# Gate preparation of an mLSTM kernel on 80 rows, and its state decay as a step of its own

## The chip, the cores and the metric

The kernel runs on one core of one Trainium2 chip. The metric is the device time of one execution in microseconds. TensorE (PE), VectorE (DVE), ScalarE (ACT), GpSimd (POOL) and SyncE (SP) work side by side, and semaphores order them.

## The reference

Three layers follow each other. The first is an mLSTM attention over 2 batches, 8 heads, 768 steps and 40 channels a head; then come two dense blocks on 1536 tokens of 320 channels.

```
for t in range(S):
    m_new = max(f[t] + m, i[t])
    f_stab, i_stab = exp(f[t] + m - m_new), exp(i[t] - m_new);  m = m_new
    C = f_stab * C + i_stab * outer(v[t], k[t])
    n = f_stab * n + i_stab * k[t]
    y[t] = sigmoid(o[t]) * (C @ q[t]) / max(abs(n . q[t]), 1)
x = rows of y                      # 1536 x 320
x = (((x @ w1) * (x @ w2)) @ w3) @ w_out        # inner width 1024
h = x @ w_in                                    # inner width 2048
out = (h * tanh(softplus(h))) @ w_out2
```

## The kernel before, in words

The sequence is cut into 6 chunks of 128 steps. A unit is one chunk of one batch with all 8 heads, so there are 12 units; two chunks form a block of 512 tokens, and the dense layers work on 3 blocks. Inside a chunk the recurrence is written as products: E builds the exponents of the weights (lines 624 and, for the first `mu` = 8 units, a product that adds the causal mask, line 623; later units are masked by GpSimd in `ms`, line 634). `dw` takes exp of them, S is the product of keys and queries (line 650), `wg` multiplies both on VectorE, and Y (line 699) applies the result to the values. What earlier chunks contribute goes through a state `st`: I (line 661) applies the state to the queries, `Ie` scales the result with `eT`, and `cb` adds Y. U (line 675) makes what the unit adds to the state. `state()` first multiplies the old state with the decay `d` (which `dx` computes from a row of I) and then adds U, all on VectorE. `vw` (GpSimd) scales the values for U. `r1` to `r3`, `xs` and `xo` make the output row, X turns it over, and `Xe` and `Xl` split it into a high and a low part.

The gates are prepared in `start()`, in three stages: chunk 0, chunk 1 and chunks 2 to 5. Sixteen sequences of (batch, head) lie on 128 rows, eight times repeated, since E needs them at several row ranges: a scan gives the running maximum m (`pa`, line 879), two subtractions make the exponents (`pt`), a clamp and a scan sum them up (`pb`, `pc`, line 900). `lr` and `ll` write the sums L as a high and a low part to rows 64 to 127, `less`, `la` and `lb` (lines 927, 931, 935) write the left factor `ex_l` of E, `rb` and `rc` the right factor `ex_r` (VectorE or ScalarE), `turn` transposes L and `turned` takes exp of it into `eT` (lines 943 and 947).

The dense layers run in fp32r with three products of high and low parts. Each weight piece comes in by a load (`raw`), and is split on ScalarE, VectorE and GpSimd (lines 487 to 512 and the `lo` step); A and B are the products with w1 and w2 (line 1057), W makes w3 times w_out ahead of time (line 1028), X1 applies it, H and O are the two products of the last layer (lines 1186 and 1210), which alternate in groups of 8.

The order of every instruction on every engine is written out before the kernel is built: the steps are nodes with an engine, an assumed duration, a due number, the nodes they need and the places (PSUM banks b0 to b7, SBUF slots) that they take. `Work.plan` lists them one after the other, at each step the node that is due first among those that could start soon; `DUE` holds the due numbers and `TUNE` the rest. Where the plan sees TensorE idle while units still run, it puts in fillers: `keep_warm` (line 594), a product of 512 columns into bank b0 that nobody reads. Loads are issued by SP in plan order. What `port=True` marks are steps that the plan keeps apart in time on VectorE and GpSimd.

Of the kernel before, what the change touches and what calls it, by code (L numbers as in the profile page):

```python
# [19 lines left out]
NQK = 2  # L20
# [24 lines left out]
    set_0=0.0, ld_o_0=0.6, ld_g=1.3, ld_qk_0=1.7, ld_kv_0=1.8, load_0=1.9, ld_o_1=4.6, lr_0=4.8, less_0=2.3,  # L45
    ll_0=4.5, la1_0=5.1, la0_0=5.4, rb_0=5.6, one_0=5.7, lb0_0=40.7, lb1_0=6.2, pl_1=6.1, rc_0=6.4, pl_0=18.6,
    E_0=5.8, pa_1=7.7, pr_1=15.4, pa_2=7.8, E_1=7.5, dw_0=8.0, ld_qk_1=8.7, pt_1=9.7, S_0=9.2, pt_2=9.4,
    ld_kv_1=23.2, pb_1=10.6, dw_1=7.0, pb_2=11.3, pc_1=11.4, pc_2=11.7, te_1=16.7, lr_1=11.5, turn_1=7.0,
    less_1=13.1, te_2=11.7, lr_2=24.7, less_2=13.8, load_1=14.8, turn_2=13.5, ll_2=13.9, la1_2=13.7, ll_1=14.5,
    sgm_0=14.3, ld_o_2=24.2, vw_0=4.4, lb1_2=13.6, U_0=-11.7, ld_qk_2=16.0, rb_1=11.7, wg_0=16.2, la0_2=16.4,  # L50
    sgm_1=17.3, vw_1=16.8, ld_kv_2=16.6, la1_1=16.9, st_0=17.9, Y_0=-10.7, la0_1=13.8, mag_0=16.9, lb0_2=18.8,
    lb0_1=19.0, set_1=19.1, lb1_1=-2.1, rc_1=19.4, S_1=19.3, clamp_0=20.0, rb_2=20.1, cb_0=20.6, load_2=18.4,
    E_2=18.1, wg_1=21.0, xs_0=23.9, r1_0=19.4, mag_1=20.5, E_3=22.0, ld_o_3=20.4, r2_0=17.9, bits1_0=11.3,
    dw_2=20.6, U_1=22.5, r3_0=27.8, bits2_0=25.1, Y_1=22.8, ld_qk_3=23.3, st_1=23.8, xo_0=31.7, bits_0=26.7,
    ld_kv_3=26.0, dw_3=23.6, S_2=24.4, cb_1=24.0, vw_2=24.7, r1_1=24.3, I_2=-2.3, rc_2=25.2, wg_2=26.2, U_2=27.2,
    xs_1=31.5, dx_2=25.6, dup_0=23.1, Ie_2=29.8, hi_0=26.6, E_4=28.1, load_3=16.7, st_2=38.2, Y_2=28.6, dw_4=29.5,
    r2_1=28.5, lo_0=28.6, r3_1=29.2, mag_2=24.8, clamp_1=29.0, xo_1=29.9, X_0=13.8, ld_qk_4=30.2, cb_2=28.4,
    E_5=24.6, Xe_0=29.1, clamp_2=24.8, dup_1=32.5, r1_2=29.7, Xl_0=24.4, xs_2=30.9, S_3=32.8, dw_5=29.1,
    ld_kv_4=62.5, r2_2=27.1, bits1_2=28.7, ld_o_4=32.5, I_3=33.4, r3_2=32.2, vw_3=33.1, bits2_2=27.0, X_1=47.3,
# [1287 lines left out]
```

## Time and profile before

| | us |
|---|---|
| median of 3 runs | 418.37 (418.22 to 418.58) |
| the profiled execution | 418.2 |
| its span, first to last instruction | 416.5 |
| TensorE busy | 409.5 (98%) |
| VectorE busy | 291.1 (70%) |
| ScalarE busy | 197.7 (47%) |
| GpSimd busy | 80.4 (19%) |

The 70% of VectorE is a mean over unlike stretches. In the first 110 us, where the units run, it is busy nearly all the time; from 300 us on it has little to do. The chain of waits that ended last is 93% TensorE and 5% VectorE, and VectorE's share of it lies in the first 20 us, and a little around 70 us.

### The profile page before, as it was taken

How to read it: one execution, taken by the hardware profiler on the slowest of the kernel's cores; microseconds unless marked ns; L12 is line 12 of the kernel's file. 1: busy time of each engine (PE TensorE's matmuls, PEld its weight loads, DVE VectorE, ACT ScalarE, POOL GpSimd, SP SyncE). 2: the span in 40 equal slices, each digit the busy share in tenths (PEclk: the TensorE clock that was granted, in tenths of full speed). 3: DMA queues.
4: the chain of work that ended last, by engine and by line, in shares of the span. 5: the costliest groups of instructions: out<-in, count | busy, mean ns of one | idle time of the engine just before them, and what ended most of it. 6: DMA issues, size and time to landing. Idle time of an engine off the chain costs nothing.

```text
span 416.5 us, 7129 instructions
## 1 busy us (share of the span) xinstructions
PE 409.5 (98%) x2815; PEld 359.8 (86%) x2815; DVE 291.1 (70%) x527; ACT 197.7 (47%) x381; POOL 80.4 (19%) x78
## 2 busy tenths in 40 slices
...
GB/s 238 324 178 220 239 119 153 139 97 127 114 50 102 168 136 101 150 139 166 65 104 87 64 127 90 164 63 2 65 0 2 0 2 2 63 2 0 2 2 64
DMA packets 30497, 40.88 MB, mean 98 GB/s; under 512 B 1856, under 2 KB 24640, under 8 KB 30464
## 3 DMA queue, kind: packets, MB, share of 16 engines
...
q10 hardware_dynamic: 512, 0.48, 0.4%
...
## 4 chain that ended last, share of the span: by engine, by line
PE 93%; DVE 5%; DMA 1%; ACT 0%; issue 0%; DVEq 0%
PE pso L1210 21%; PE psh L1186 20%; PE psb L1057 11%; PE psa L1057 10%; PE psw L1028 7%; PE psY L699 5%; PE psS L650 3%; PE psx L1097 3%; PE psx L1099 3%; PE psx L1098 3%; PE psI L661 2%; PE psx L1102 1%; PE psx L1101 1%; PE psE L624 1%; DVE gates L410 1%; PE psX L743 1%
## 5 line engine op out<-in xcount | busy, mean ns | idle before, releaser
L410 DVE TENSOR_TENSOR gl<-u,gh 128x512 fp32r<-128x512 f32 x48 | 32.9, 691 | 68.7 <-ACT u L1195 68.7
L1191 ACT ACTIVATE gh<-psh 128x512 fp32r<-128x512 f32 x48 | 28.8, 601 | 79.5 <-PE psh L1186 79.4
L1186 PE MATMUL psh<-xd,wih 64*128 64x512 f32 x240 | 59.4, 395 | 0.0
L1186 PEld LDWEIGHTS psh<-xd,wih 64*128 64x128 f32 x240 | 43.1, 184 | 3.6 <-ACT u L1195 0.2
L1210 PE MATMUL pso<-wo,gh 128*128 128x320 f32 x192 | 42.6, 310 | 0.0
L1186 PE MATMUL psh<-hs,wih 64*128 64x512 f32 x144 | 41.6, 395 | 0.0
L502 DVE SCALAR_TENSOR_TENSOR f<-raw,f 128x640 int32<-128x640 int32 (+2 forms) x44 | 40.0, 908 | 0.9
L507 DVE SCALAR_TENSOR_TENSOR f<-raw,f 128x640 int32<-128x640 int32 (+2 forms) x44 | 37.7, 858 | 0.9
L410 POOL TENSOR_TENSOR th<-f,th 128x512 fp32r<-128x512 f32 x16 | 22.1, 1381 | 62.1 <-ACT th L512 59.1
L1210 PEld LDWEIGHTS pso<-wo,gh 128*128 128x128 f32 x192 | 32.0, 188 | 1.1 <-issue 1.1
L1186 PE MATMUL psh<-xd,wil 64*128 64x512 f32 x120 | 31.6, 391 | 0.0
L1186 PE MATMUL psh<-hs,wil 64*128 64x512 f32 x120 | 31.4, 391 | 0.0
L1210 PE MATMUL pso<-wo2h,gh 128*128 128x320 f32 x96 | 30.0, 312 | 0.0
L1210 PE MATMUL pso<-wo2h,gl 128*128 128x320 f32 x96 | 29.6, 309 | 0.0
L1210 PE MATMUL pso<-wo2l,gh 128*128 128x320 f32 x96 | 29.6, 309 | 0.0
L1210 PE MATMUL pso<-wo,gl 128*128 128x320 f32 x96 | 29.6, 309 | 0.0
L1057 PE MATMUL psa<-hs,w12h 128*128 128x512 f32 x72 | 28.9, 401 | 0.1
L1195 ACT ACTIVATE u<-psh 128x512 f32<-128x512 f32 x48 | 28.9, 603 | 0.0
L1057 PE MATMUL psb<-hs,w12h 128*128 128x512 f32 x72 | 28.3, 394 | 0.2 <-DVE y L410 0.2
L1186 PEld LDWEIGHTS psh<-hs,wih 64*128 64x128 f32 x144 | 25.7, 184 | 3.2 <-issue 1.3
L1028 PE MATMUL psw<-woh,th 128*128 128x320 f32 x128 | 28.5, 310 | 0.0
L493 DVE TENSOR_SCALAR f<-f 128x640 f32<-128x640 f32 (+2 forms) x44 | 23.6, 536 | 7.0 <-ACT f L487 6.3
...
## 6 DMA issues: line engine op xcount, KB each, us to landing
...
```

The source lines that it names most:

```text
L410: return eng.tensor_tensor(out=o, in0=a, in1=b, op=op)
L493: nc.vector.tensor_scalar(out=ff, in0=ff, scalar1=HI_MIN, scalar2=HI_MAX, op0=ALU.max, op1=ALU.min)
L502: nc.vector.scalar_tensor_tensor(out=f, in0=t["raw"][:, :, 1], scalar=-0x40000000, in1=f, op0=ALU.bitwise_and, op1=ALU.bitwise_or)
L507: nc.vector.scalar_tensor_tensor(out=f, in0=t["raw"][:, :, 0], scalar=29, in1=f, op0=ALU.logical_shift_right, op1=ALU.bitwise_or)
L650: nc.tensor.matmul(t["S"][g][:, p * T:(p + 1) * T], lhsT=t["qk"][rows, 1, p, :], rhs=t["qk"][rows, 0, p, :], start=True, stop=True)
L699: nc.tensor.matmul(ps[:, h * VW:(h + 1) * VW], lhsT=t["w"][:, h, :], rhs=t["v"][:, h, :], start=True, stop=True)
L1028: nc.tensor.matmul(ps, lhsT=t[a][:, 0, c * 128:(c + 1) * 128], rhs=wo[b], start=(c0 + c + s == 0), stop=(c0 + c == KC - 1 and s == 2))
L1057: nc.tensor.matmul(ps, lhsT=a, rhs=b, start=(n == 0 and not begun), stop=(n == len(seq) - 1))
L1186: nc.tensor.matmul(mt[i + k]["ps"], lhsT=w[k][:, c], rhs=x[k][c], start=(n == 0 and c == 0), stop=(n == 2 and c == KC2 - 1))
L1191: nc.scalar.activation(out=t["gh"], in_=t["ps"], func=AF.Mish)
L1195: nc.scalar.activation(out=t["u"], in_=t["ps"], func=AF.Mish)
L1210: nc.tensor.matmul(ps, lhsT=t[a][:, sl], rhs=wo[b], start=(ft == 0 and n == 0), stop=(ft == KF2 - 1 and n == 2))
```

## The change

The gates of chunk 0 stay as they were. For chunks 1 to 5 the running maximum is one scan over 640 columns on the 16 distinct rows. Then each (chunk, sequence) gets a row of its own, 80 rows of 128 columns: the gates are loaded a second time in this form (`cf`, `ci`), and the maxima are placed on the 80 rows by five products with a selecting matrix (`mv`, into PSUM). Subtractions, clamp, sum and `less` run once on 80 rows. The results are split in high and low parts (`chi`) and placed back on the rows that E needs by products with a second selecting matrix (`rp`, in groups of two chunks), from where ScalarE and VectorE copy them out of PSUM (`evL`, `ev0`, `ev1`). One transpose replaces five. The loads of the gates of chunks 1 to 5 are four transfers in place of two, of 16 or 80 rows in place of 128.

The decay of the state becomes the node `sd`; `ENG` puts it on GpSimd for units 2 to 9, the units that have one. `r2` of unit 5 goes to GpSimd as well. `mu` is 9, so one more unit takes the causal mask from TensorE. The plan gets a bonus `fb` for a TensorE node of the same form as the one before, fills idle time to 0.901 rather than 0.972, and adds fillers where a stretch would have too few wide products (`gd` = 0.26). A unit's Y is listed behind X of four units earlier. In the last block the slots of the second layer's results may also lie in buffers that are free by then, and the output tiles take others. `DUE` is new for most early nodes, and the added nodes have entries. With `ss` = 9 and `grp` = (0, 8, ..., 48) S stays one node a unit and H and O alternate in groups of 8. The old stages' functions, shown above, are gone; below are the added lines and those of the old ones that they replace elsewhere.

```diff
-    sgg=(2, 4), mu=8, s_pe=0.268, s_act=0.543, s_dve=0.435, s_pool=0.206, ahead=1, w0n=5, ff=0.972, gd=0.0,
+    sgg=(2, 4), mu=9, s_pe=0.268, s_act=0.563, s_dve=0.435, s_pool=0.1, ahead=1, w0n=5, ff=0.901, gd=0.26,
     ph=0.071, a0=-12.81, ap=-93.853, a_ld=-1652.39, e_e=8363.2, e_s=3345.95, e_r=2252.59, g_ld=6316.58,
...
+                    stay = TUNE["fb"] if e == "PE" else 0.0
+                    c = min((c for c in cand if c[0] <= s0 + TUNE.get(SLACK.get(e), 0.0)),
+                            key=lambda c: c[1] - (stay if self.form[c[2]] == form else 0.0))
...
+        if tag[0] == "y":
+            k, n = divmod(int(tag[1:]), 5)
+            h, l = xset["b", k]
+            return (h[:, n] if n < 3 else l[:, n - 3]).bitcast(F32)
...
+        sd_e = ENG.get(f"sd{u}", ENG["sd"])
+
+        def sd():
+            s = st[b].rearrange("a p (e v) -> a (p e) v", e=2)
+            tt(nc.gpsimd if sd_e == "POOL" else nc.vector, s, s, t["d"].unsqueeze(2).to_broadcast([128, H, VW]), mult)
+
         def state():
...
-            if c > 0:
-                s = st[b].rearrange("a p (e v) -> a (p e) v", e=2)
-                tt(nc.vector, s, s, t["d"].unsqueeze(2).to_broadcast([128, H, VW]), mult)
...
+        g = (c - 1) // 2 if c else 0
+        node("E", "PE", -K["e_e"], 0.92 if pe_mask else 0.46, E, [(f"ev{b}" if c else f"lb{b}", g), ("rb", c), ("rc", c), ("E", u - 1)],
...
-                node("dx", "ACT", -1, 0.08, dx, [("I", u)], [(places("d", 2), [("st", u)])], table=["exp"])
+                node("dx", "ACT", -1, 0.08, dx, [("I", u)], [(places("d", 2), [("sd", u)])], table=["exp"])
+                node("sd", sd_e, -1, pool(328) if sd_e == "POOL" else dve(328), sd, [("I", u), ("dx", u)], port=True)
             st_a = c == 0 and ENG["st0"] == "ACT"
-            node("st", "ACT" if st_a else "DVE", -1, 2 * act(164) if st_a else (dve(328) if c else 0.0) + 2 * dve(164), state,
-                 [("U", u), ("I", u), ("dx", u)])
-        node("Y", "PE", 0, 1.8, Y, [("wg", u), ("ld_kv", u)], [at("cb")], warm=0.31)
+            node("st", "ACT" if st_a else "DVE", -1, 2 * act(164) if st_a else 2 * dve(164), state,
+                 [("U", u), ("sd", u)] if c else [("U", u)])
+        node("Y", "PE", 0, 1.8, Y, [("wg", u), ("ld_kv", u), ("X", u - 4)], [at("cb")], warm=0.19)
...
+        CF = 1
+        NK = NCH - CF
+        S1 = S - CF * T
+        NC = G * NK
...
+        m, one, L, sel_m = part(gb, S + 1, T, F, 2 * NC - G)
+        cf, ci, cL = [x[0:NC] for x in part(gc, T, T, T)]
+        chi = z_a.tile([128, N], F32R, tag="z3", name="split", bufs=1)[0:NC]
+        sel_m = sel_m[0:G]
         L2 = xs.tile([128, 2, N], F32R, tag="ls2", name="gates", bufs=1).rearrange("a c n -> a (c n)")[:, 0:S]
+        sel_r = z_a.tile([128, N], F32R, tag="z2", name="sel", bufs=1)[0:NC, 0:176]
...
+        def prep_sel():
+            nc.gpsimd.memset(sel_m, 0.0)
+            nc.gpsimd.tensor_copy(out=sel_m[:, NC - G:NC], in_=ident[0:G, 0:G])
+            nc.gpsimd.memset(sel_r.bitcast(F32), 0.0)
+            for a in range(0, NC, 32):
+                r = slice(a, min(a + 32, NC))
+                n = r.stop - a
+                nc.gpsimd.tensor_copy(out=sel_r[r, 32:160].rearrange("a (h q) -> a h q", h=2)[:, :, 0:n],
+                                      in_=ident[r, r].unsqueeze(1).to_broadcast([n, 2, n]))
...
+        def gate_max(c):
+            a, z = c * T, (c + 1) * T
+            nc.vector.tensor_tensor_scan(out=m[:, a + 1:z + 1], data0=f[:, a:z], data1=i[:, a:z], initial=m[:, a:a + 1],
+                                         op0=add, op1=ALU.max)
+
+        def gate_diff(f, i, m_before):
+            tt(nc.vector, f, f, m_before, add)
+            tt(nc.vector, i, f, i, sub)
+
+        def gate_sum(f, i, L, skip=0):
+            nc.vector.tensor_scalar(out=f, in0=i, scalar1=0.0, scalar2=-120.0, op0=ALU.min, op1=ALU.max)
+            nc.vector.tensor_tensor_scan(out=L[:, skip:], data0=one[0:L.shape[0], skip:], data1=f[:, skip:], initial=0.0,
+                                         op0=mult, op1=add)
+
+        def less(i, L):
+            nc.vector.scalar_tensor_tensor(out=i, in0=i, scalar=0.0, in1=L, op0=ALU.max, op1=add)
+
+        def cut(a, c):
+            return a[:, c * T:(c + 1) * T]
+
+        gate_max(0)
+        gate_diff(cut(f, 0), cut(i, 0), cut(m, 0))
+        nc.vector.memset(L[:, 0:1], 0.0)
+        gate_sum(cut(f, 0), cut(i, 0), cut(L, 0), 1)
+
+        def ld_c():
+            for o, a in ((f1, f_gate), (i1, i_gate)):
+                nc.sync.dma_start(out=o, in_=a[0:G, F:S])
+            for o, a in ((cf, f_gate), (ci, i_gate)):
+                nc.sync.dma_start(out=o, in_=by_chunk(a[0:G, F:S]))
+
+        gps = {}
+
+        def mv():
+            gps["m"] = bank("psg")
+            for c in range(NK):
+                a = F + c * T
+                nc.tensor.matmul(gps["m"][0:NC, 0:T], lhsT=sel_m[:, NC - G - c * G:2 * NC - G - c * G], rhs=m[0:G, a:a + T],
+                                 start=(c == 0), stop=(c == NK - 1))
+
+        def group(n):
+            return range(2 * n, min(2 * n + 2, NK))
+
+        def rp(n):
+            gps["r", n] = bank("psg")
+            r = slice(32 * n, min(32 * n + 32, NC))
+            for c in group(n):
+                o = gps["r", n][:, c % 2 * 2 * T:(c % 2 + 1) * 2 * T]
+                for e in range(2):
+                    a = 32 + c % 2 * G - 32 * e
+                    nc.tensor.matmul(o, lhsT=sel_r[r, a:a + 128], rhs=chi[r, 2 * e * T:2 * (e + 1) * T], start=(e == 0), stop=(e == 1))
+
+        def copied(n, k):
+            w = len(group(n))
+            o = slice(F + 2 * n * T, F + (2 * n + w) * T)
+            return o, gps["r", n][:, 0:2 * w * T].rearrange("a (c k t) -> a c k t", c=w, k=2)[:, :, k]
+
+        def flat(o):
+            return o.rearrange("a (c t) -> a c t", t=T)
+
+        def ev_eng(nm, n):
+            return ENG[f"{nm}{n}"]
+
+        def evL(n):
+            sl, a = copied(n, 0)
+            o, a = flat(L2[64:128, sl]), a[64:128]
+            nc.scalar.copy(o, a) if ev_eng("evL", n) == "ACT" else nc.vector.tensor_copy(out=o, in_=a)
+
+        def ev(b, n):
+            sl, a = copied(n, 1)
+            o, a = flat(ex_l[b][0:64, sl]), a[0:64]
+            if ev_eng(f"ev{b}", n) == "ACT":
+                nc.scalar.activation(out=o, in_=a, func=AF.Copy, scale=neg_b[:, b:b + 1])
+            else:
+                nc.vector.tensor_scalar_mul(out=o, in0=a, scalar1=neg_b[:, b:b + 1])
...
+        def turn():
+            gps["t"] = bank("psg")
+            nc.tensor.transpose(gps["t"][:, 0:NC], cL, ident[:NC, :NC])
+
+        def turned():
+            nc.scalar.activation(out=eT[:, CF:NCH].rearrange("a c g -> a (c g)"), in_=gps["t"][:, 0:NC], func=AF.Exp)
...
+        add_node(("ld_c",), "SP", -K["g_ld"] + 1, 1.6, ld_c, bytes=164e3)
...
+        add_node(("ps", 0), "POOL", due - 3, 1.6, prep_sel, port=True)
+        add_node(("pa", 1), "DVE", due, scan(S1), lambda: nc.vector.tensor_tensor_scan(
+            out=m[0:G, F + 1:S + 1], data0=f1, data1=i1, initial=m[0:G, F:F + 1], op0=add, op1=ALU.max), [("ld_c",)], port=True)
+        add_node(("mv", 1), "PE", due, 1.1, mv, [("pa", 1), ("ps", 0)], [(AT, [("pt", 1)])], warm=0.3)
+        add_node(("pt", 1), "DVE", due, 2 * dve(T), lambda: gate_diff(cf, ci, gps["m"][0:NC, 0:T]), [("mv", 1)])
+        add_node(("pc", 1), "DVE", due, dve2(T) + scan(T), lambda: gate_sum(cf, ci, cL), [("pt", 1)], port=True)
+        add_node(("less", 1), "DVE", due + 1, dve(T), lambda: less(ci, cL), [("pc", 1)], port=True)
+        for k, (nm, nl, a, x) in enumerate((("lr", "ll", cL, "pc"), ("la", "lb", ci, "less"))):
+            h, l = chi[:, k * T:(k + 1) * T], chi[:, (2 + k) * T:(3 + k) * T]
+            add_node((nm, 1), "ACT", due, act(T), lambda h=h, a=a: nc.scalar.copy(h, a), [(x, 1)])
+            add_node((nl, 1), "DVE", due, dve(T), lambda h=h, l=l, a=a: tt(nc.vector, l, a, h.bitcast(F32), sub), [(nm, 1)], port=True)
+        for n in range((NK + 1) // 2):
+            w = len(group(n))
+            add_node(("rp", n), "PE", due, 0.26 * w, lambda n=n: rp(n), [("ll", 1), ("lb", 1)],
+                     [(AT, [("evL", n), ("ev0", n), ("ev1", n)])], warm=0.5)
+            for nm, fn in (("evL", lambda n=n: evL(n)), ("ev0", lambda n=n: ev(0, n)), ("ev1", lambda n=n: ev(1, n))):
+                e = ev_eng(nm, n)
+                add_node((nm, n), e, due, act(w * T) + 0.1 * (nm != "evL") if e == "ACT" else dve(w * T), fn,
+                         [("rp", n)] + ([("pl", int(nm[2]))] if nm != "evL" else []))
+        add_node(("te", 1), "PE", due, 0.2, turn, [("pc", 1)], [(AT, [("turn", 1)])], warm=0.0)
+        add_node(("turn", 1), "ACT", due, 0.16, turned, [("te", 1)], table=["exp"])
...
+        GP = places("z", 16) + (places("z", 6, 25) + places("y", 10)) * last
+        YP = places("z", 16) if last else places("z", 6, 25)
...
```

## Rows read from the trace of the kernel before

**Rows 1.** The page: span, TensorE's line of section 1, engines in section 4.

```profile
span 416.5 us, 7129 instructions
...
PE 409.5 (98%) x2815; PEld 359.8 (86%) x2815; DVE 291.1 (70%) x527; ACT 197.7 (47%) x381; POOL 80.4 (19%) x78
...
PE 93%; DVE 5%; DMA 1%; ACT 0%; issue 0%; DVEq 0%
```

**Rows 2.** Windows: start:end, length, busy us of each engine, clock, DMA share.

```profile
10.00:20.00 10.00, 9.18 (x73) 6.92 (x73) 9.67 (x22) 7.44 (x15) 2.29 (x2) 1.00 1.02 321
...
300.00:400.00 100.00, 100.00 (x772) 91.25 (x769) 25.10 (x40) 35.35 (x69) 0.00 (x0) 1.00 0.03 11
```

**Rows 3.** Windows of the filler product psz alone: length, busy us, (count).

```profile
20.00:30.00 10.00, 0.98 (x3) 0.48 (x3) 1.00 0.56 180
30.00:40.00 10.00, 1.17 (x4) 0.68 (x4) 1.00 0.77 225
```

**Rows 4.** Timeline of TensorE, 7 to 27 us: start, duration, what.

```profile
9.85 1.16 PE L650 MATMUL psS<-qk 40*128 40x128 f32 x16
...
12.28 0.51 PE L675 MATMUL psU<-vw,kv 128*40 128x41 f32 x16
...
14.80 0.42 PE L943 MATMUL psg<-ident,gates 16*128 16x16 f32 x4
...
17.94 2.18 PE L699 MATMUL psY<-kv,w 128*128 128x41 f32 x16
...
22.15 0.50 PE L623 MATMUL psE<-causal,identr 128*128 128x512 f32 x1
22.49 0.40 PE L624 MATMUL psE<-ex_r,ex_l 128*128 128x512 f32 x1
22.72 0.39 PE L623 MATMUL psE<-causal,identr 128*128 128x512 f32 x1
...
25.59 1.10 PE L661 MATMUL psI<-st,qk 128*128 128x82 f32 x8
26.48 0.25 PE L664 MATMUL psI<-ex_r,ones 128*128 128x8 f32 x1
```

**Rows 5.** Timeline of VectorE, 7 to 24 us.

```profile
7.87 1.81 DVE L879 TENSOR_TENSOR_SCAN gates<-gates 128x128 f32<-128x128 f32 x2
...
15.53 0.69 DVE L410 TENSOR_TENSOR ex_r<-gates,sel_h 64x512 fp32r<-64x512 f32 x1
16.25 0.74 DVE L935 SCALAR_TENSOR_TENSOR ex_l<-gates,neg_b,ex_l 32x512 fp32r<-32x512 f32 x1
17.02 1.29 DVE L410 TENSOR_TENSOR w<-psS,w 128x512 f32<-128x512 f32 x2
...
18.91 0.34 DVE L935 SCALAR_TENSOR_TENSOR ex_l<-gates,neg_b,ex_l 32x128 fp32r<-32x128 f32 x1
```

**Rows 6.** Groups of VectorE by shape, 0 to 120 us: busy us, mean ns.

```profile
L410 DVE TENSOR_TENSOR st<-st,d 128x328 f32<-128x328 f32 x8 | 4.4, 548 | 0.3 <-ACT d L639 0.3
...
L879 DVE TENSOR_TENSOR_SCAN gates<-gates 128x512 f32<-128x512 f32 x1 | 1.3, 1285 | 0.0
```

**Rows 7.** Timeline of GpSimd, 0 to 75 us, with the idle time before.

```profile
10.51 1.22 POOL L410 TENSOR_TENSOR vw<-kv,w 128x328 f32<-128x328 f32 x1 [5.82 <-DMA kv<-in_kv_dram]
16.52 1.07 POOL L410 TENSOR_TENSOR vw<-kv,w 128x328 f32<-128x328 f32 x1 [4.79 <-DMA kv<-in_kv_dram]
...
41.89 0.74 POOL L410 TENSOR_TENSOR vw<-kv,w 128x328 f32<-128x328 f32 x1
...
57.01 1.37 POOL L634 TENSOR_SCALAR_AFFINE_SELECT w<-w 128x1016 f32<-128x1016 f32 x1 [2.79 <-ACT w L629]
```

**Rows 8.** Timeline of SyncE's queue, 0 to 50 us.

```profile
2.18 0.43 SPq L833 DMA_DIRECT2D gates<-in_f_gate_dram  x1
```

**Rows 9.** Timeline of VectorE, 56 to 66 us.

```profile
56.44 0.95 DVE L507 SCALAR_TENSOR_TENSOR f<-raw,f 128x768 int32<-128x768 int32 x1
57.31 1.88 DVE L502 SCALAR_TENSOR_TENSOR f<-raw,f 128x768 int32<-128x768 int32 x1
```

More of the change, by code (lines that the diff above doesn't have):

```diff
@@ L41 @@
+    lo_w126='DVE', lo_w127='POOL',
 )
 DUE = dict(
[L45 to L59, printed above, removed]
@@ new lines @@
+    ll_0=-1.9, la1_0=-6.3, la0_0=-6.5, rb_0=4.1, one_0=5.7, lb0_0=36.9, lb1_0=2.1, pl_1=6.5, rc_0=0.6, pl_0=-14.5,
+    E_0=5.8, pa_1=7.7, pr_1=10.3, E_1=-13.1, dw_0=8.4, ld_qk_1=8.7, pt_1=2.0, S_0=9.5, ld_kv_1=23.6, dw_1=7.0,
+    pc_1=1.3, te_1=12.8, lr_1=-6.8, turn_1=13.0, less_1=10.0, load_1=13.9, ll_1=13.8, sgm_0=14.3, ld_o_2=24.6,
+    vw_0=5.0, U_0=-11.7, ld_qk_2=16.4, rb_1=4.0, wg_0=16.5, sgm_1=17.3, vw_1=16.8, ld_kv_2=16.9, st_0=17.9,
+    Y_0=-10.7, mag_0=16.9, set_1=19.1, rc_1=18.3, S_1=19.3, clamp_0=15.4, rb_2=21.8, cb_0=20.6, load_2=18.8,
@@ L938, in start @@
-        gps = {}
-        def turn(c0, c1):
-            ps = gps[c0] = bank("psg")
-            for c in range(c0, c1):
-                nc.tensor.transpose(ps[:, c * G:(c + 1) * G], L[0:G, c * T:(c + 1) * T], ident[:G, :G])
-        def turned(c0, c1):
-            p3 = gps[c0][:, c0 * G:c1 * G].rearrange("a (c g) -> a c g", g=G)
-            nc.scalar.activation(out=eT[:, c0:c1], in_=p3, func=AF.Exp)
-        for f0 in (pa, pt, pb, pc):
-            f0(0, 1)
-        add_node(("ld_g",), "SP", -K["g_ld"], 0.4, lambda: ld_g(1, NCH), bytes=660e3)
@@ new lines, in start @@
+        for b in range(B):
+            add_node((f"la{b}", 0), "ACT", due, act(T) + 0.1, lambda b=b: la(b), [("less", 0)])
+            add_node((f"lb{b}", 0), "DVE", due, dve(T), lambda b=b: lb(b), [(f"la{b}", 0)], port=True)
+        due = K["g1"]
+        for b in range(B):
+            add_node(("pl", b), ENG["prep"], due - 2, act(640) if ENG["prep"] == "ACT" else 0.75,
+                     lambda b=b: prep_l(b, T, S, ENG["prep"]))
+        add_node(("pr", 1), ENG["prep"], due - 1, act(1024) if ENG["prep"] == "ACT" else 1.2,
+                 lambda: prep_r(1, ENG["prep"]))
@@ L1154, with group @@
     MH = places("b", 4)
-    GP, UP, YP = places("z", 16), places("z", 4, 16), places("z", 6, 25)
+    UP = places("z", 4, 16)
+    def group(i):
+        return next((a, b) for a, b in zip(K["grp"], K["grp"][1:]) if a <= i < b)
     acc = {}
```

263 lines of the change are left out of this document (116 added, 147 removed).

## The prediction

> **What bounds the kernel now.** I read the page first, then the windows, then each engine's timeline of the first 27 us. The page gives TensorE 98% of a 416.5 us span, and 93% of the chain that ended last [rows 1]. The windows say where it is not at its limit: from 300 to 400 us it is busy 10 of 10 at the full granted clock, while VectorE has a quarter of its time; at 10 to 20 us 0.8 us is missing and VectorE is at 9.7 of 10 [rows 2]. A busy TensorE is not always useful: psz is the filler product that only holds the clock. Its windows show 3 fillers at 20 to 30 us and 4 at 30 to 40 [rows 3].
>
> So the time is TensorE's useful work plus fillers and gaps, and almost all of those lie at the start. From the first score product (9.85) to the first Y (17.94) pass 8.09 us. Useful in them: S 1.16, U 0.51, five transposes of L about 0.5 (four take 0.42) [rows 4]; 5.9 us are filler or idle. After that come the 7 fillers, at the 0.23 us of a 512-column product (22.49 to 22.72 [rows 4]) 1.6 us: 7.5 us are wasted behind 9.85. The whole gain must come out of these and out of cheaper work.
>
> What holds Y back is VectorE: from 7.87 it works through the gates of chunks 1 to 5 until 17.0; only then does wg of unit 0 run (17.02), though its scores were complete at 11. More gate work follows from 18.91 on [rows 5].
>
> **The change, part by part.** *Gates, VectorE.* Gone: 7.87 to 17.02 less one ex_r of 0.69 that stays, 8.5 us; and two ex_l at 0.34, the 32-row subtraction 0.69 and an ex_l of 0.74 behind 18.91, 2.1 us: 10.6 together [rows 5] (the shapes of the later ones are those of the rows shown). Added: one scan over 640 columns. 512 take 1.285 and the pair of scans 1.81 [rows 5, 6], so 128 take about 0.5 and a column 2.1 ns: 1.55 us. The rest is 128 columns wide on 80 rows where it was 512 wide. A 128-wide ex_l takes 0.34, a 512-wide one 0.74 [rows 5], on 32 rows both; I take 0.34 for each 128-wide step and 0.5 for its scan: two subtractions 0.68, clamp and sum 0.84, less 0.34, two low parts 0.68, three copies out of PSUM of up to 256 columns 1.0 (the other six on ScalarE; 0.74 each as the upper bound). Sum 5.1, at most 6.3; VectorE is relieved of 5.5. This counts an instruction by its columns and not by its rows: the decay's 328 columns on 128 rows take 0.548 [rows 6], between the two of 32 rows.
>
> *Gates, TensorE.* Added: mv, 5 fp32 products of 128 columns. No row shows one; the I product, 82 columns, takes 0.89 for 4 (25.59 to 26.48 [rows 4]), so 5 cost 1.1 at that width and 1.7 scaled by columns; I take 1.2, nearer the row. rp, 10 fp32r products of 256 columns: 0.12 each by half of the 0.23, at most the whole 0.23: 1.2 to 2.3; I take 1.4. One transpose instead of 5: -0.4. One more unit with the mask product (mu 9): 2 x 0.23 = 0.46. Together +2.6 (2.3 to 4.4), of it mv surely where TensorE now runs fillers.
>
> *Where Y and E land.* The gates of chunk 0 are the same steps, so E_0, E_1 and S_0 stay up to 11.0. The scan runs 7.87 to 9.45, mv beside S_0 until 12.1, the subtractions and sums until 13.5; the planner may put wg_0 (1.3) ahead of or between them: Y_0 at 12 to 13.5, where it was 17.94. Low parts by 14.5, rp 15, copies 15.8, two ex_r of 0.69: E_2 at 17.2; it was at 22.15 [rows 4]. Both shift by about 5.
>
> *Loads.* Gates of chunks 1 to 5 fall from 655 KB to 164 KB. At the 321 GB/s of 10 to 20 us, where the DMA engines are full [rows 2], 0.49 MB is 1.5 us. That is needed: vw of units 0 and 1 wait for kv, until 10.51 and 16.52 [rows 7]. SP issues four transfers in place of two, all before sg, qk and kv: at most 0.9 us of its queue if an issue takes 0.43 [rows 8]. Net: kv about 0.5 to 1.5 earlier, kv_1 at 15 to 16. Two waits are new on VectorE: the subtractions wait for mv, and behind them in its queue stand wg_0, clamp and sum, for which Y_0 waits; the copies of rp wait for TensorE, and behind them stand the two ex_r, for which E_2 waits. Both are in the times of the part above.
>
> *Decay on GpSimd.* VectorE loses 8 x 0.548 = 4.4 us [rows 6]. GpSimd pays 0.74 alone [rows 7], up to 1.22 beside VectorE: 6 to 10 us on an engine that is at 19%. The link I, dx, decay, st grows by 0.2 to 0.7 and one hop; I take 0 on the path, since the next unit of the same batch is one chunk on. The row speaks for a smaller relief, though: while GpSimd ran 57.01 to 58.4, VectorE's 768-wide operation took 1.88 where the one before took 0.95 [rows 7, 9].
> The Trainium skill (GPSIMD Engine Reference, Specifications) says that GpSimd's memory interfaces are shared with VectorE and contend with instructions that have two SBUF inputs, as the decay and most conversions have; the trace agrees in the doubled 1.88. By it the decay's own 0.74 on GpSimd could take as much from VectorE as the 0.548 it saves there: relief zero; its time is that of rival B.
>
> *Order anew.* Two products of unlike form cost 0.11 more at the seam (22.15 to 22.49 is 0.34, 22.49 to 22.72 is 0.23 [rows 4]). The planner now favours staying in a form. With 12 S and 10 U blocks it could save between nothing and some 14 seams, 1.5 us; I take -0.3. Against it stands the guard (gd 0.26) that adds fillers where few wide products run: 0 to 8 at 0.23, inside the waste below. The grouping of 8 in the second part stays; more slots in the last block cost and give nothing, as TensorE has no gap at 300 to 400 [rows 2]. ss=9 leaves S per unit. r2 of one unit on GpSimd: nothing.
>
> **Sum.** Waste after: from 9.85 to 17.2, 7.35 us, of which useful S_0 1.1, mv 1.2, U_0 0.44, te 0.2, Y_0 1.8, S_1 1.1, some rp 0.9 = 6.7; 0.7 left, and I take 1.2 as they won't pack without holes. Later fillers 1.1 of today's 1.6, VectorE being freer. 2.3 - 7.5 + 2.6 - 0.3 = -2.9. The profiled execution took 418.2 (span 416.5 and 1.7 around it), next to the median 418.37: 415.3.
>
> **The rivals.**
> *A, larger gain.* Seams and later fillers go almost wholly: waste 1.1, work +2.3, seams -1.5 gives -5.6: 412.6. For it: 9.9 us less on a VectorE at 9.7 of 10. Against: fillers are placed by a plan, not by need. 0.16.
> *B, decay buys nothing.* The relief of 4.4 is eaten because VectorE's operations lengthen beside GpSimd, as the 1.88 shows; later waste grows to 2.2 rather than falling to 1.1: 416.4. For it the 1.88, against it VectorE operations that read PSUM beside GpSimd. 0.12.
> *C, the start is bound elsewhere.* kv_1 and ScalarE hold Y_1 and E_2 (vw_1 waited for kv until 16.52 [rows 7]); the freed 5 us are filled with fillers and the guard adds some: waste 5, so -0.2: 418.0. 0.12.
> *D, slower.* The decay queues on GpSimd, in order, behind a vw that waits for kv (4.79 us before 16.52, 5.82 before 10.51 [rows 7]) or behind xs and xo. Then st is late, the I of the next chunk is late, and TensorE, which has no other work before block 0 is done, stands. At 0.8 us for each of 8 decays it costs 6.4: waste 2.3 + 6.4 = 8.7, +3.5: 421.7. It decides above 2.9 us in all, 0.4 us a decay. Against it: vw waits mostly early, and chunks are some 10 us apart. 0.18.
>
> **How the numbers follow.** Forecast 0.42, its own range 413.3 to 417.2; A 0.16, B 0.12, C 0.12, D 0.18. A measurement tells 0.2% (0.84 us) from no change. Faster: forecast, A, B and a third of C, 0.74; same 0.08; slower D, 0.18. The range, 412.0 to 419.2, leaves out most of D and a little of A.
>
> **What would show it.** Right: Y_0 at 12 to 13.5 and E_2 near 17; one scan of 640 near 1.55; ten narrow products of rp within 2.3 us; fewer than 10 fillers behind 10 us; TensorE 10 of 10 from 18 us on; the start of the second part's first product 3 us earlier. Wrong: gaps in front of I that end with st, a granted clock below 1.00 in the first 20 us, VectorE operations longer beside GpSimd, or Y_0 behind 15.

## The result, and the profile after

The changed kernel takes 421.93 us (median of 11 runs, 418.80 to 423.27) against 418.34 before: ratio 1.0071 [1.0054, 1.0089]. Forecast were 415.3 us and a range of 412.0 to 419.2; the kernel became 3.6 us slower. Ratios, here and below, leave out runs over 1.5% above the fastest of the same kernel; two of the kernel before are such (426.4 and 426.8). The eleven runs of the changed kernel differ by the granted clock that each had: 418.80 and 418.92 at 1.00, 420.71 to 421.93 at 0.992 to 0.996, 422.25 to 423.27 at 0.986 to 0.988. So two things need a cause: at full clock the expected gain is missing (about +0.5 instead of -2.9), and most runs lose another 2 to 4 us to the clock, where nine of the eleven runs of the kernel before took 418.15 to 418.58. The profiled execution took 420.71 us.

The page of the kernel after, its span and section 1, beside [rows 1]:

```profile
span 419.0 us, 7157 instructions
...
PE 412.5 (98%) x2828; PEld 361.6 (86%) x2828; DVE 285.1 (68%) x508; ACT 196.8 (47%) x382; POOL 84.0 (20%) x92
```

VectorE has 6.0 us less to do, TensorE 3.0 us more (part of it products at a lower clock, see below). The windows after, by 10 us, then 300 to 400 us (length, busy time of PE, PEld, DVE, ACT and POOL with instruction counts, granted clock, DMA share, GB/s), beside [rows 2]:

```profile
0.00:10.00 10.00, 7.69 (x23) 5.44 (x23) 7.37 (x19) 7.22 (x14) 5.11 (x20) 1.00 0.56 154
10.00:20.00 10.00, 9.77 (x95) 8.09 (x95) 4.96 (x13) 7.06 (x13) 1.49 (x2) 0.99 1.03 312
20.00:30.00 10.00, 10.00 (x64) 8.21 (x64) 7.84 (x16) 7.35 (x18) 1.58 (x3) 0.67 0.72 225
```

```profile
300.00:400.00 100.00, 100.00 (x774) 90.35 (x775) 26.07 (x43) 33.56 (x65) 0.00 (x0) 1.00 0.04 14
```

Between 10 and 20 us VectorE fell from 9.67 to 4.96, as planned. From 20 to 30 us the granted clock is 0.67: TensorE ran at half speed (1.2 GHz) for part of it, and "busy 10.00" hides that, since a product at half clock is busy for twice as long. From 300 to 400 us nothing has changed. The fillers (psz alone: PE, PEld), beside [rows 3]:

```profile
0.00:10.00 10.00, 7.47 (x22) 5.25 (x22) 1.00 0.56 154
10.00:20.00 10.00, 1.41 (x5) 0.89 (x5) 0.99 1.03 312
20.00:30.00 10.00, 1.70 (x3) 0.69 (x3) 0.67 0.72 225
30.00:40.00 10.00, 0.48 (x1) 0.19 (x1) 1.00 0.61 188
```

The kernel before, from 0 to 20 us:

```profile
0.00:10.00 10.00, 5.86 (x12) 3.66 (x12) 1.00 0.77 231
10.00:20.00 10.00, 5.43 (x19) 3.25 (x19) 1.00 1.02 321
```

Five of 19 are left between 10 and 20 us. Ahead of 10 us they rose from 12 to 22, in front of E_0, which is fed later now. TensorE's timeline, beside [rows 4]:

```profile
10.08 0.47 PE L635 MATMUL psE<-ex_r,ex_l 128*128 128x512 f32 x1 [0.52 <-DVE ex_l L1017]
...
11.88 1.31 PE L960 MATMUL psg<-gates 16*80 16x128 f32 x10
13.12 1.16 PE L662 MATMUL psS<-qk 40*128 40x128 f32 x16
...
15.99 0.31 PE L714 MATMUL psY<-kv,w 128*128 128x41 f32 x2
16.45 1.75 PE L714 MATMUL psY<-kv,w 128*128 128x41 f32 x14 [0.15 <-DVE w L417]
18.14 0.75 PE L973 MATMUL psg<-split,sel 32*128 32x256 f32 x8
18.81 1.27 PE L662 MATMUL psS<-qk 40*128 40x128 f32 x16
20.02 0.79 PE L973 MATMUL psg<-split,sel 16*128 16x256 f32 x2
...
22.64 1.97 PE L673 MATMUL psI<-st,qk 128*128 128x82 f32 x8
...
24.55 0.77 PE L634 MATMUL psE<-causal,identr 128*128 128x512 f32 x1
...
27.41 1.87 PE L714 MATMUL psY<-kv,w 128*128 128x41 f32 x16
```

Two more lines of the kernel before, the starts of E_2 and Y_1:

```profile
19.95 0.48 PE L623 MATMUL psE<-causal,identr 128*128 128x512 f32 x1
...
23.71 2.05 PE L699 MATMUL psY<-kv,w 128*128 128x41 f32 x16
```

S_0 begins at 13.12, not at the 9.85 where it stood; Y_0 at 15.99 (before 17.94), E_2 at 24.55 (before 19.95), Y_1 at 27.41 (before 23.71). What starts at 22.15 in [rows 4] is E_3: each unit has two pairs of E products, those of E_2 stand at 19.95 to 20.73, and E_3 follows S_1. The I block that took 1.10 takes 1.97: half clock. VectorE's timeline shows where the freed time went, beside [rows 5]:

```profile
8.03 1.54 DVE L1045 TENSOR_TENSOR_SCAN gates<-gates 16x640 f32<-16x640 f32 x1
9.59 0.34 DVE L1017 SCALAR_TENSOR_TENSOR ex_l<-gates,neg_b,ex_l 32x128 fp32r<-32x128 f32 x1
13.23 0.28 DVE L417 TENSOR_TENSOR gates<-gates,psg 80x128 f32<-80x128 f32 x1 [3.30 <-PE psg L960]
...
18.82 0.56 DVE L504 TENSOR_SCALAR f<-f 128x768 f32<-128x768 f32 x1 [1.53 <-ACT f L498]
...
20.01 0.48 DVE L997 TENSOR_SCALAR ex_l<-psg,neg_b 64x256 fp32r<-64x256 f32 x1
```

VectorE is idle: 3.30 us until the placed maxima come from TensorE, then 1.53 us at the head of a queue whose first entry waits for ScalarE, while the copies that E_2 needs stand behind it. And the 0.34 us step for E_0 stands behind the 1.54 us scan; by that E_0's second product starts at 10.08. SyncE's queue, beside [rows 8]:

```profile
1.25 0.41 SPq L950 DMA_DIRECT2D gates<-in_f_gate_dram  x1
1.71 0.42 SPq L950 DMA_DIRECT2D gates<-in_i_gate_dram  x1
2.17 0.96 SPq L952 DMA_DIRECT2D gates<-in_f_gate_dram  x1
3.19 0.74 SPq L952 DMA_DIRECT2D gates<-in_i_gate_dram  x1
...
5.74 0.35 SPq L598 DMA_DIRECT2D kv<-in_kv_dram  x1
```

The two 80-row loads hold the queue for 0.96 and 0.74 us, about twice the 0.43 of a load of [rows 8]. From 3 to 5 us the DMA engines moved 29 GB/s, where they had moved 268 before, and kv of unit 0 is issued at 5.74, where it was 3.92.

### The profile page after: what moved, and what is told of

Read it like the earlier page. It is cut to its first block, busy times and chain, and to the rows that moved or that the text cites. A ratio compares the mean times of both kernels' runs of the same rounds, so it can differ in the third digit from the quotient of the medians.

```text
span 419.0 us, 7157 instructions
## 1 busy us (share of the span) xinstructions
PE 412.5 (98%) x2828; PEld 361.6 (86%) x2828; DVE 285.1 (68%) x508; ACT 196.8 (47%) x382; POOL 84.0 (20%) x92
## 3 DMA queue, kind: packets, MB, share of 16 engines
HBM read 37.96 MB, written 1.97 MB: 95 GB/s over the span
## 4 chain that ended last, share of the span: by engine, by line
PE 95%; DVE 2%; ACT 2%; issue 0%; ACTq 0%; DVEq 0%
PE pso L1300 20%; PE psh L1276 20%; PE psa L1142 11%; PE psb L1142 11%; PE psw L1113 7%; PE psY L714 5%; PE psS L662 3%; PE psx L1182 3%; PE psx L1183 3%; PE psx L1184 3%; PE psI L673 2%; PE psE L635 2%; PE psx L1187 1%; PE psx L1186 1%; PE psE L634 1%; PE psX L760 1%
## 5 line engine op out<-in xcount | busy, mean ns | idle before, releaser
L417 DVE TENSOR_TENSOR gl<-u,gh 128x512 fp32r<-128x512 f32 x42 | 29.5, 714 | 63.3 <-ACT u L1285 63.1
L1281 ACT ACTIVATE gh<-psh 128x512 fp32r<-128x512 f32 x42 | 25.2, 600 | 74.5 <-PE psh L1276 74.5
L498 ACT ACTIVATE f<-raw 128x512 f32<-128x512 f32 (+2 forms) x28 | 21.2, 757 | 15.1 <-POOL th L417 9.1
L417 POOL TENSOR_TENSOR wil<-f,wih 128x640 fp32r<-128x640 f32 x8 | 13.5, 1691 | 66.1 <-ACT wih L523 66.1
L1276 PE MATMUL psh<-ls,wih 64*128 64x512 f32 x96 | 26.3, 390 | 0.0
```

Source lines behind the costliest of these rows:

```text
L417: return eng.tensor_tensor(out=o, in0=a, in1=b, op=op)
L498: nc.scalar.activation(out=t["f"].bitcast(F32), in_=t["raw"][:, :, 1].bitcast(F32), func=AF.Abs)
L1276: nc.tensor.matmul(mt[i + k]["ps"], lhsT=w[k][:, c], rhs=x[k][c], start=(n == 0 and c == 0), stop=(n == 2 and c == KC2 - 1))
L1281: nc.scalar.activation(out=t["gh"], in_=t["ps"], func=AF.Mish)
```

## The experiments

Except for one, all start from the changed kernel's own written-out order and move single steps in it, or change the lines shown, so that everything else stays put. In the diffs, which show the lines that matter, a number beside a step is its place in that order (about its planned microsecond); `ADD` (p, n) puts in n products psz at place p, and `FILLS` p: n sets how many stand there. Runs of the kernel before, taken beside each experiment, had medians from 418.37 to 418.51, and the ratios are against these.

**Is it E_0's late step?**

```diff
+ MOVE = {("lb0", 0): 8.33}   # the 0.34 us step of batch 0, ahead of the scan over 640
+ FILLS = {3.57: 12}          # 12 fillers ahead of E_0 in place of 17
```

> The changed kernel with two edits in its listed order, all else in the same order: ex_l of batch 0 in chunk 0 is listed ahead of the 640-column scan on VectorE, and 12 fillers instead of 17 stand in front of E_0. Theory S (the freed VectorE time is lost at the start, because E_0 now waits for a step behind the scan): E_0's second product starts near 8.4 instead of 10.08, Y_0 near 14.5 instead of 16.0, and the time falls by 1.2 to 1.8 us against the changed kernel at the same granted clock. Theory K (the loads bound the start: kv of unit 1 comes at 17.1): E_0 and Y_0 are earlier but E_2 and everything behind it stay within 0.4 us, and more time runs at the lower clock.

Measured 422.19, 1.0078 [1.0056, 1.0100]. E_0's product starts at 9.24 instead of 10.08 and Y_0 at 15.09, and the median gains nothing: five of six runs have a granted clock of 0.988 to 0.990. At 0.988 its runs take 422.02 to 422.30, the changed kernel's 422.29 to 423.27, so up to 1 us may lie in the earlier step; it goes to a longer stretch at half clock (10.2 us in the profiled run, 6.8 in the changed kernel's).

**Is it the clock?**

```diff
+ ADD = [(18.60, 3), (19.64, 3), (21.0, 3)]   # 9 more fillers, around S_1 and U_1
```

> The changed kernel in its own order with 9 more fillers: 3 ahead of rp of the first group, 3 ahead of S_1, 3 ahead of U_1. Theory C (the clock: TensorE is at 1.2 GHz from 19.7 to 26.6 because narrow products with few fillers stand there): mean clock back to 0.998, and the time near 418.8 to 419.5 in nearly every run, with a narrow spread, although 2.1 us of fillers were added. Theory S or D (the clock is a side effect, the time is lost by late steps): the time rises by up to 2 us to 422 to 424, spread as wide as before.

Measured 420.05, 1.0033 [1.0021, 1.0046]; all six runs lie within 0.2 us at a clock of 0.998 to 1.0. Its window, in the columns of above:

```profile
20.00:30.00 10.00, 10.00 (x94) 8.12 (x92) 7.85 (x16) 8.50 (x22) 2.23 (x3) 1.00 0.72 226
```

Nine products that compute nothing make the kernel 1.9 us faster: the same 10 us hold 94 products, where the changed kernel at 0.67 had 64. Against the changed kernel's own two runs at full clock (418.80 and 418.92) they cost 1.2 us. The new plan numbers are not what took the fillers out: by the kernel's own plan the old ones (`ff` 0.972, `gd` 0) would put in three more up to 45 us, one of them behind 10 us, and the guard `gd` puts in none (worked out from the plan, not run). The counterpart takes fillers from the kernel before, 3 in place of 19 between S_0 and Y_0:

```diff
+ FILLS = {10.0: 1, 12.03: 0, 12.94: 0, 14.56: 2}   # base: the kernel before
```

> The kernel before in its own order with 3 instead of 19 fillers between S_0 and Y_0. If these fillers were only waste (as the prediction counted them): no change, 418.2 to 418.6, since TensorE waits there anyway. Theory C (they hold the clock): the granted clock falls below 0.995 in most runs and the time rises by 1.5 to 3.5 us, to 420 to 422.

Measured 425.24, 1.0157 [1.0108, 1.0206]. Its windows:

```profile
10.00:20.00 10.00, 6.04 (x49) 4.39 (x47) 9.69 (x22) 7.67 (x15) 2.03 (x2) 0.75 1.03 330
20.00:30.00 10.00, 10.00 (x64) 8.00 (x63) 6.40 (x13) 6.11 (x12) 1.56 (x2) 0.57 0.45 152
```

TensorE was busy 6.04 of 10 us, its clock fell (0.75, then 0.57), and the kernel lost 6.8 us in the median (four runs, 422.51 to 428.06) by leaving out work that does nothing; 1.5 to 3.5 had been expected. The Trainium skill (TensorE: Matmul & The Clock Gate, HAM oscillation) describes a kernel whose short bursts of products are followed by longer waits for loads, and whose clock falls back at each such wait. In e4 TensorE did stand still for 3.96 of 10 us, though mostly for VectorE and not for loads. In the changed kernel the clock fell too, at 19.73, and there TensorE had been busy 9.77 of 10 us. So a full busy column did not mean that the clock was safe.

**Does the decay on GpSimd cost or gain?** Twice: on the changed order, and on e2 with its clock held.

```diff
- tt(nc.gpsimd if sd_e == "POOL" else nc.vector, s, s, t["d"]...
+ tt(nc.vector, s, s, t["d"]...
```

> The changed kernel in its own order with the decay computed on VectorE instead of GpSimd, at the same place of the order. Theory D (the decay on GpSimd is what slows it: GpSimd's queue, or VectorE lengthened beside it): the time falls by more than 1 us. If the decay is off the path: within 0.8 us of the changed kernel, 421 to 422.5; VectorE has 4.4 us more to do, and if VectorE were the bound between 20 and 110 us the time would rise by 1 to 4 us.

Measured 419.73, 1.0036 [1.0015, 1.0058]; at a clock of 1.00 its runs take 418.6 to 419.1, the changed kernel's 418.8 and 418.9. Its median is lower because half of its runs hold the clock. Whether the place of the decay changes how often it is held isn't shown: five of ten runs hold it here, two of eleven of the changed kernel.

> The base of e2 with the decay on VectorE at the same place of the order; it measures the decay without the spread of the clock. Theory D (the decay on GpSimd costs TensorE something): falls by more than 0.8 us, below 419.2. Off the path: 419.7 to 420.5. The prediction's view (it relieves VectorE, and VectorE is short of time): it rises by 0.5 to 2 us.

Measured 419.81, 1.0025 [1.0014, 1.0036], against e2's 420.05: with the clock held, taking the decay back to VectorE makes the kernel 0.24 us shorter, if anything (the intervals overlap; one run far off, at 1766.48, is left out). The offload buys nothing. e3's page, and its group of decays on VectorE:

```profile
span 416.9 us, 7158 instructions
...
PE 409.9 (98%) x2828; PEld 359.9 (86%) x2828; DVE 287.2 (69%) x516; ACT 196.6 (47%) x382; POOL 76.4 (18%) x84
```

```profile
L417 DVE TENSOR_TENSOR st<-st,d 128x328 f32<-128x328 f32 x8 | 4.8, 609 | 0.4 <-ACT d L650 0.4
```

VectorE's total is 287.2 us, so 282.4 without the decays; with them on GpSimd it is 285.1 (the changed kernel's page). Of 4.8 us moved away, 2.7 came back as longer VectorE operations, nearly all in two groups of steps of 768 columns on the weights.

**Do the loads hold the second unit?** Both from e2: q, k and v ahead of weight pieces and of the 80-row gates; then the same with e6's order below.

```diff
+ MOVE = {("ld_o", 0): 3.01, ("ld_qk", 1): 3.02, ("ld_kv", 1): 3.03, ("ld_o", 1): 3.04,
+         ("load", 0): 3.06, ("ld_kv", 2): 14.83, ("ld_o", 2): 14.9, ("load", 1): 15.5}
+ # and the two loads of the 80-row gates issued behind kv of unit 0
```

> The changed kernel with the 9 added fillers of e2 (420.05 us, its base) and another order of the loads alone: q, k and v of units 0 and 1 ahead of the first weight piece, the two 80-row gate loads behind v of unit 0, v of unit 2 ahead of the second piece. Theory K (the loads bound the start: four gate transfers put kv_0 at 5.74 in SyncE's queue where it was 3.92, and DMA is full from 10 to 20 us): kv_1 is there by 14 instead of 17, qk_2 no longer holds I_2, and the time falls by 0.7 to 2 us to 418 to 419.4. Theory Q (the order on VectorE and ScalarE bounds it: E_2 waits for gate copies queued behind weight work and for cb_0): within 0.4 us of 420.05.

Measured 421.04, 1.0052 [1.0035, 1.0070], clock 1.00: 1.0 us slower than e2. The loads did come earlier: vw of unit 1 ran at 12.72, in e2 at 17.34. But E_2 stayed at 24.80 and Y_1 came at 27.45, no earlier than in e2 (24.82 and 26.77). So the loads were not what held the second unit there.

> Both edits, on the base of e2. If loads and order each hold the start in turn (K and Q), this falls below either alone: 415 to 417.5, faster than the kernel before. If only one of them counts, it equals that one within 0.4 us. If the time is lost later (neither), all three stay within 0.5 us of 420.05.

Measured 420.01, 1.0035 [1.0014, 1.0056]. Its five runs at a clock of 0.998 to 1.0 take 419.14 to 419.30, 0.55 above the 418.56 to 418.77 of eight of e6's ten runs (below); the other five lose the clock and take 420.73 to 435.72. That is below e2 but not below e6: the two don't add up. Loads in this order cost 0.5 to 1.0 us in both pairs.

**Can the earlier gates be used?** From e2, the steps up to E_2 reordered: the copies out of PSUM and the two ex_r ahead of the weight work on VectorE and ScalarE, E_0's step ahead of the scan, 9 fillers ahead of E_0, E_2 ahead of I_2.

```diff
+ MOVE = {("lb0", 0): 8.33, ("lb", 1): 15.45, ("rp", 0): 16.5, ("rp", 1): 16.6, ("ev0", 0): 17.0,
+         ("rb", 1): 17.1, ("rc", 1): 17.2, ("cb", 0): 17.3, ("sgm", 0): 16.9, ("E", 2): 20.9, ...}
+ FILLS = {3.57: 9}
```

> The changed kernel with the 9 added fillers of e2 and another order of the steps that lead to E_2 alone: ex_l of batch 0 ahead of the 640-column scan (8 fillers fewer ahead of E_0), the last split ahead of wg_0, the first two rp ahead of Y_0, their copies ahead of the sigmoid and of the first weight piece, cb_0 behind them, E_2 ahead of I_2. Theory Q: E_2 starts at 20 to 21 instead of 24.8 and the time falls by 1.5 to 4 us, to 416 to 418.5. Theory K: E_2 is earlier, but Y_1, I_2 and the rest wait for kv_1 (17.1) and qk_2 (22.8), and the gain is under 1 us.

Measured 418.70, 1.0000 [0.9988, 1.0012], clock 0.998 to 1.0 in all ten runs. TensorE's timeline, from a run that took 419.76, 1.1 us above the median:

```profile
20.65 0.51 PE L640 MATMUL psE<-causal,identr 128*128 128x512 f32 x1
...
21.70 1.65 PE L611 MATMUL psz<-causal,identr 128*128 128x512 f32 x5
24.69 1.09 PE L679 MATMUL psI<-st,qk 128*128 128x82 f32 x8 [1.35 <-DMA qk<-in_qk_dram]
...
26.70 1.87 PE L720 MATMUL psY<-kv,w 128*128 128x41 f32 x16
```

E_2 is 4 us earlier than in e2 (24.82), and Y_1 is where it was (26.70, e2 26.77): five fillers and a wait for unit 2's load take its place (how long the wait is in the faster runs wasn't seen). It is still 0.7 later than in the kernel before (19.95). The next four experiments follow that wait.

```diff
+ MOVE += {("wg", 1): 22.2, ("Y", 1): 22.25, ("E", 3): 22.30, ("dw", 3): 22.5, ("cb", 1): 24.55}   # e9, from e6
```

> Base: e6_gates_first. The second unit's Y_1 and E_3 are issued ahead of I_2 instead of behind it (and wg_1, dw_3 and cb_1 with them), so that TensorE works on them while the qk load of unit 2 is under way. Nothing else is changed. Theory P (at full clock the time is TensorE's own sum of products, fillers and idle; a step that comes earlier pays only what filler or idle goes with it): Y_1 starts at about 22.9 instead of 26.7, the 1.35 us wait of I_2 for its load is gone, time 417.2, 1.2 to 1.8 below e6. Rival L (a later stage holds the end, as the loads or the weights' preparation): Y_1 earlier by 3 to 4 us and the time within 0.4 of e6's 418.7.

Measured 427.64, 1.0178 [1.0128, 1.0228]. One of six runs, at a clock of 0.995, took 421.42. In the profiled run (429.23) Y_1 starts at 23.2 as expected and I_2 no longer waits, but TensorE is idle for 1.1 us until Y_2 has its weights at 31, and the clock falls:

```profile
30.00:40.00 10.00, 8.77 (x46) 7.59 (x46) 8.29 (x19) 4.89 (x10) 5.45 (x6) 0.62 0.60 181
40.00:50.00 10.00, 10.00 (x66) 9.50 (x66) 3.96 (x10) 4.19 (x12) 2.27 (x4) 0.50 0.44 134
```

It stays down from 32.37 to 52.85 us. My theory had no place for this.

```diff
+ FILLS = {21.44: 0}; ADD = [(22.31, 4)]      # e11, from e9: 11 fillers out, 4 in
+ MOVE += {("wg", 1): 19.9, ("clamp", 0): 20.1, ("bits1", 0): 20.15, ("st", 1): 20.7}
```

> e9_y1_first with the fillers around S_1 and ahead of Y_1 taken out (11 fillers less, 4 put in behind E_3) and wg_1 and st_1 ahead of the clamp and the bits of the weight in VectorE's list. Theory P: S_1 at about 18.2, Y_1 at 20.9 to 21.5, 7 fillers of 0.23 us less: 1.0 to 1.6 us below e9, about 415.9, if the granted clock stays at 1.00. Rival C (the fillers were what held the clock): a stretch at half clock appears between 15 and 30 us, mean clock 0.99 or less, and the time is 1 to 4 us above e9's.

Measured 422.46, 1.0088 [1.0069, 1.0107], clock 0.991 in three of six runs, 0.990 in one; two lose more and take 431.6. That is rival C's half clock; its time was set against an e9 that lost more itself. Y_1 starts at 20.74, 3 us ahead of the kernel before, and Y_2 at 31.23, behind it (29.94). VectorE:

```profile
27.18 0.50 DVE L423 TENSOR_TENSOR y<-psI,eT 128x328 f32<-128x328 f32 x1 [4.85 <-PE psI L682]
...
28.07 0.95 DVE L519 SCALAR_TENSOR_TENSOR f<-raw,f 128x768 int32<-128x768 int32 x1
29.05 1.46 DVE L524 SCALAR_TENSOR_TENSOR f<-raw,f 128x768 int32<-128x768 int32 x1
30.43 0.19 DVE L745 RECIPROCAL r<-r 128x8 f32<-128x8 f32 x1
30.55 1.23 DVE L423 TENSOR_TENSOR w<-psS,w 128x512 f32<-128x512 f32 x2
```

It stood idle for 4.85 us behind an eviction that waits for I_2, with 2.4 us of weight work behind it in the list; that then ran just when Y_2's weights (the last row) were due.

```diff
+ MOVE += {("bits2", 0): 22.0, ("bits", 0): 22.1, ("wg", 2): 27.75}   # e12, from e11
+ ADD = [(22.24, 2), (22.31, 4), (30.0, 4)]                           # e13: also (18.6, 3), (19.64, 3)
```

> e11_y1_early with the two operations on the first weight's bits (0.95 us and 0.95 to 1.46 us on VectorE) issued into VectorE's idle stretch ahead of I_2's eviction instead of behind it, wg_2 straight behind S_2, and 6 fillers: 2 ahead of Y_1, 4 ahead of Y_2. Theory P: the 1.1 us wait of Y_2 for wg_2 is gone (Y_2 at 29.5 to 30.0 with the fillers, where e11 had 31.2 and e6 31.4), and if the granted clock holds at 1.00 the time is 416.8 to 417.6. Rival C: there are fewer fillers ahead of 22 us than in e6, and a stretch at half clock stays, with 420 or more. Rival L (a later stage holds the end): clock 1.00 and 418.3 to 418.9 all the same.

Measured 418.23, 1.0001 [0.9986, 1.0016], the lowest median of a kernel with these gates. Seven of eleven runs hold a clock of 0.998 to 1.0 and take 417.93 to 418.27, median 418.16. The kernel before, at such a clock in 18 runs beside them, took 418.07 to 418.71, median 418.4: that is 0.2 us less, between theory P and rival L. Four runs lose the clock and take 419.1 to 423.9. The profiled one is among them; its clock fell behind 17.5 us, though TensorE's busy column is full:

```profile
10.00:20.00 10.00, 10.00 (x109) 8.30 (x107) 7.59 (x18) 6.41 (x14) 2.29 (x3) 0.89 1.03 320
```

> e12 with the 6 fillers around S_1 back (3 ahead of rp_2, 3 ahead of S_1; 1.4 us of TensorE). Theory P: the clock is held as in e6, Y_1 at about 23, Y_2 at about 30.5, time 417.0 to 418.0, a little below the kernel before. Rival L: 418.3 to 418.9. Rival C: a stretch at half clock all the same, 420 or more.

Measured 419.30, 1.0024 [1.0014, 1.0033]; nine of its twelve runs lie within 0.12 us, one took 420.78, and two lie far above (453.75 and 2301.26). The nine hold the clock, at 0.998 to 1.0, and their time is 1.1 us above e12's runs that hold it: 0.19 for each of the six fillers. None of the three expectations had 419.3.

**What do the selecting products cost?** Each done twice into the same bank, the result the same; on e9 and on e2.

```diff
- for c in range(NK):                 + for c in 2 * list(range(NK)):                         # mv
- for c in group(n):                  + for c in [c for c in group(n) for _ in range(2)]:     # rp
```

> e9_y1_first with every selecting product of the gates (the 5 of mv and the 5 of rp, two passes each or two halves each) done twice over into the same bank, to the same result: TensorE's psg work goes from 2.4 us to about 4.6 us at full clock. Theory P: 2.0 to 2.4 us more than e9, about 419.5: the selecting products are paid in full. Rival H (they lie in gaps that fillers or waits would fill anyway): within 0.5 of e9. In between: mv (1.2 us, ahead of S_0) is paid and rp (1.0 us, ahead of S_1) is not, or the reverse; the start of Y_0 tells which.

Measured 429.75, 1.0275 [1.0242, 1.0309], clock 0.971 to 0.983. With e9's own clock down as well the pair tells nothing.

> Base: e2_more_fill, whose clock stays up. Every selecting product of the gates is done twice over into the same bank, to the same result. psg's TensorE time goes from 2.4 to about 4.6 us. Theory P (paid in full, ahead of S_0 and of S_1): 2.0 to 2.4 us more than e2, about 422.2, with the clock at 1.00. Rival H (they fill gaps): 420.0 to 420.5.

Measured 423.87, 1.0115 [1.0084, 1.0146]; its two runs at a clock of 0.999 take 422.39 and 422.45, 2.4 above e2's 420.05; the other two lose the clock (425.28 and 432.73). A second set of selecting products is paid in full, even where fillers stand beside it. That the first set is paid alike is inferred from it.

## Why the prediction was wrong

The time missed the forecast by 6.6 us: 3.1 by the clock, 3.5 at full clock.

**The step that failed is the sum's first term.** "7.5 us are wasted behind 9.85", filler or idle, of which 5.2 were to go (2.3 - 7.5). It had two faults.

*The clock had no price.* A filler there was not all waste: it held the clock for S, U and Y around it. e2 (nine fillers more, 1.9 us faster) and e4 (sixteen fewer in the kernel before, 6.8 us slower) show it from both sides. The prediction named "a granted clock below 1.00 in the first 20 us" as a sign of being wrong, but no term or rival priced it, and the guard that the prediction had adding fillers put in none. In the median that is about 3.1 us (421.93 against the 418.80 and 418.92 at full clock).

*At full clock the waste moved instead of going.* Behind 10 us the fillers fell from 26 to 11, ahead of it they rose from 12 to 22, while E_0's step stood behind the scan. Up to 60 us that is 38 and 33, about 1.2 us at the 0.23 of [rows 4]. Nor did idle time fall: e3's profiled run, at full clock and with the changed kernel's order on TensorE, has 416.9 - 409.9 = 7.0 us of it, the kernel before 416.5 - 409.5 = 7.0. So of the 5.2 us only 1.2 came.

**The added work was right.** The psg products alone, 0 to 60 us, in the kernel before (PE, PEld, ACT) and in e2 (PE, PEld, DVE, ACT), which has the changed kernel's products at full clock:

```profile
0.00:60.00 60.00, 0.65 (x5) 0.46 (x5) 0.41 (x2) 1.00 0.72 219
```

```profile
0.00:60.00 60.00, 2.83 (x21) 2.06 (x21) 1.58 (x4) 2.32 (x7) 1.00 0.69 211
```

That is +2.2 for mv, rp and the transposes, as predicted (1.2 + 1.4 - 0.4); that it comes out exactly is partly luck, as mv took more (1.31) and rp less. The upper bound of the added work, 4.4, should be 4.1 by its own terms. With the mask's 0.46 and 1.2 less of fillers, TensorE's busy time would grow by 1.5 us; e3 shows 0.4 (409.9 against 409.5). The other 1.1, where the prediction had 0.3 for the order anew, was not taken apart.

**"E_0, E_1 and S_0 stay up to 11.0" failed.** This is where the fillers ahead of 10 us come from. Two pieces of new work stood in front: the scan, listed ahead of E_0's step, and mv, which TensorE ran ahead of S_0 and not "beside" it; S_0 began at 13.12. Y_0 came at 15.99 instead of 12 to 13.5.

**E_2 at 17.2 failed by more.** The prediction had read E_2's old start as 22.15, which is E_3's; E_2 stood at 19.95, so the gain it put at 5 us was 2.8 at most. The copies stood behind weight work that waits for ScalarE, and E_2 came at 24.55. e6 mended most of that (20.65) and got the kernel level with the one before, but no further: each wait removed uncovered the next, qk of unit 2 in e6, VectorE's list in e11. Rival C, a start bound elsewhere at 418.0, comes nearest to what remains at full clock, but by its number only: of its two causes, e5 shows that kv of unit 1 did not hold Y_1. Why e12 at full clock equals the kernel before and doesn't beat it stays open: the 2.2 us of psg fit, but the profile of e12 fell into a run that lost the clock, so what pays these 2.2 us back was not seen.

**Right were most sizes.** The scan over 640 took 1.54 (1.55 predicted); two 80-row steps 0.28 and 0.29 (0.34); VectorE's 10 to 20 us lost 4.7. VectorE's total fell by 6.0, not 9.9: 2.7 came back beside GpSimd, and without the decays it fell by 4.3 (from 291.1 - 4.4 to 282.4) where 5.5 were forecast. **The decay's 0 on the path was right**, and rival D's queue on GpSimd did not appear: with the decay back on VectorE the time is the same at full clock. Rival B's mechanism is real, but off the path. The Trainium skill (GPSIMD Engine Reference, Specifications) says that GpSimd shares its SBUF interfaces with VectorE and contends with VectorE instructions that have two SBUF inputs. The trace agrees, with 2.7 of 4.8 us taken back; that is not the whole relief, as rival B had it, and none of it showed in the time.

**Loads.** "At most 0.9 us of SP's queue" took an issue at 0.43; the 80-row ones took 0.96 and 0.74, and kv of unit 0 was issued 1.8 us later. vw of unit 1 ran at 17.14 instead of 16.52 [rows 7]: the load it waits for came later, not earlier.
